# Forty unread matmuls and a new order of the first 337 steps in a linear-attention and ELU kernel

## The chip, the cores and the metric

The kernel runs on one core of one Trainium2 chip. The metric is the time of one execution on the device, in microseconds (us). Engines are named as in the profile: PE is TensorE (its weight loads are PEld), DVE is VectorE, ACT is ScalarE, POOL is GpSimd, SP is SyncE. Each engine works through its own instructions in order; semaphores make one wait for another.

## What is computed

Queries, keys and values have 8 batches, 8 heads, 576 positions and 64 dimensions. Queries and keys go through a feature map of 2 x 128 exponentials, attention is linear in these features, and the result of all heads, one row of 512 per position, goes through two dense layers with an ELU between them.

```python
def phi(x):
    proj = np.einsum('bhsd,df->bhsf', x, w_phi)
    proj = proj - np.max(np.abs(proj), axis=-1, keepdims=True)
    return np.concatenate([np.exp(proj), np.exp(-proj)], axis=-1)
q_p, k_p = (phi(q), phi(k))
kv = np.einsum('bhsf,bhsd->bhfd', k_p, v)
z = np.sum(k_p, axis=2)
out = einsum('bhsf,bhfd->bhsd', q_p, kv) / (einsum('bhsf,bhf->bhs', q_p, z)[..., None] + 1e-06)
...
h = x @ w_in                                  # x: 4608 x 512, w_in: 512 x 2048
g = np.where(h > 0.0, h, np.exp(np.minimum(h, 0.0)) - 1.0)
return g @ w_out                              # w_out: 2048 x 512
```

## The kernel before

The work is cut into 16 groups of four heads of one batch (n = 0 to 15; groups 2b and 2b+1 belong to batch b) for the attention, and 9 chunks of 512 rows for the dense layers, each with 16 slices of the hidden width (jt). All of it runs in one interleaved stream. The string ORDER lists 1,797 steps; each letter calls the next instance of one function, a digit gives the PSUM bank (of 8) that it writes, and a star picks the other engine for a copy. The string fixes each engine's order of instructions; every data and buffer dependence becomes a semaphore wait.

The steps that matter for the first 60 us, with their letter and the line at which the profile shows them:

- a, start: loads w_phi on the queues of SP and ACT, clears mhl[0], mhl[1] and w_pad on DVE, and makes the identity on POOL. b, weights: one cast on DVE (L182), two on ACT (L187). c and d: the selection matrices on DVE (L192, L201).
- e, f, g: loads of k, q and v, issued by POOL (L209); the first batch comes in pieces. h: the two halves of w_in (L218). i: w_out (L221). POOL's loads share one queue and are served in its order; a load also waits for the one eight places before it, whose semaphore it takes over.
- j and l: PE transposes of k and q of the groups 0 to 3 (L233), in a first and a second block of the nine 128-column pieces. k and m: the copies out of PSUM (L240), on DVE, or on ACT with a star.
- A: projection of k (L287), in three thirds per group. B: two exponentials of each third on ACT (L298). C: the maxima on DVE (L305). D: exponentials of the maxima on ACT (L315). E: v times these on POOL (L324), four per group. F: two casts per group on POOL (L333).
- M: projection of q with positions on partitions (L361). N: its maxima on DVE (L388). O: the split of the maxima in two bf16 parts in mhl (L414, L415). P: their transpose (L421). Q: its copy (L426).
- S: projection of q with features on partitions, and the maxima subtracted by matmuls with the selection matrices (L469, L481). T: two exponentials on ACT (L493).
- U: kv of a group in two halves (L509), V: its copy (L519). W: features times kv (L558). X: the division on DVE (L572 to L575). Y and Z: transposes of the result and copies (L623, L633, L640), which make the columns of the dense layers' input xT; Z is on DVE, or on ACT with a star.
- p: the first dense layer for one slice (L665), in 256 columns for chunk 0 and 512 later. q: its exponential on ACT (L676), r: the minimum on POOL (L681), s: the rest of the ELU on DVE (L685). t: the second dense layer, four of its 16 matmuls at a time (L693). u, v: copy and store.

A step is named below by its letter and its instance: S1,0 is the first piece of group 1, U1,1 the second half of kv of group 1, T1,1,0 the first exponential of the second piece of group 1. Copies and divisions read PSUM; a step that writes a bank waits until all who read what was there are done. In the groups 0 and 1 the maxima of the first piece stay in their bank until the split has read them.

Of the kernel before, what the change touches and what calls it, by code (L numbers as in the profile page):

```python
# [15 lines left out]


ORDER = """
eeeacj0j5dkk*bA6CA1A3CBBBBDj0kj5kA6CCBBfl0l2BBmmM1NOgDA4BBfl0l7gmm*P1QS2TCDefA0CTM6NOhhgiEEEFFU4
EEUDM2NV*W6XBBP2Q*S4TTM0NM2NFFEU6EEUOP1Qj0j3S4kkM1NV*W6Xl0S2mTTTTl1mY5Z*Y7j6kZOP0W3XQ*S0TTA5Cp2q  # L20
rp7qM3NrssS0TTBp4qA0p3p2CBqrrsj7kl6mqrssM4Np7p3BBM0Np6A4enfDFqrsqrqBrssCp2qp0Y7p3p1rqrZ*O*qrBW6E
sssDqFrl2m*P4Q*p0p5qrXqrEEssM2Np4qrES6TM0NsS2TTTM0NsY6Zp7qrO*sA0A2BBBU4UVCp7qrsp6qrsP5QBt4S0TCp7
qrsp5p6W2XzTW0XDp7EEFqrqrqttA0nS2TTssrsCBp5qrtu*p7p2p3p4t6qrgDBszsqp5qrqS0rstrTsoFsEqp4Tp7rqzS2s
A0rTtEsCToU4qA2BUrzstV*CBW4up7XW0qBt6rXzDBM4FtNzM0M2sA4NvBp7tNqBzrA0sM2O*BCftBENP7t5uQCEDS2M6TtN
FeTS0M6ETtNTEU2S0A6UTCop4VtqTp3rzBsW0qnp4Xrp2qszW0rqu*O*p3DXvBEp5qsvrp7qrszp6rqsFsA0rqM2np4NBEp5
qCrzP3p2rQ*sqp3srqsDp7rqsfp6sqrBp5rsqEsM0qA2p4NBrt7BrsqFS0CgtTsrTS2EM5TNS0toTsTA5U2CTUBS0VvtBW2z
Tt6XTW4uzA0DXS2BtETzCtFETtzBA2M4BS0t7oTCtDTNFtEBvM0A4EM2NBtzNeBU0fu*UA2Cp6Bp5Cqut4rDBsEp7qM2V*r
p6NqEDnW0wstwrqxgM2trNW0FnetxEp5vusS0qM2Rp7syTNp6TFrqS2Rp4qsrTrsp5qsTp7rqysW0qS2xp6rTzrTp4sEzsq
A0U2qCroUrsBp7RV*syA5BCW2p4zxDqW0Eqxp3Brp2rBsRqA0S5qCnt7rTgRtsvTrstBEvsDS3M5TytNzTt2yu*BW3EzS5x
A0tBFzTRM3CtyTNFtzBEwM5S0vU3NTUToA5Vt7BuA0CtCzDtBEW2BtfxBA4p6BRyp3CqDEW0u*wp2qxrBp7FqFsrS0M4TEt6  # L30
NTtrsqtRrsM0ysM3p5NEzp7qNp2rzqsW0rqp4nxrp5qevstrsqsrS0uU2RTUy*S6TzVp4TsW0vqp3xTrp5qoRrsA0qS6p2CT
rp4TsvqsW6qp3rzBrsp5qexBt2rqRS0DA6srotBsytBsyTA3CtETCzW5Dt7FxFBEtBnRM0yA5M3NBztEutNBzEM0wU2CvfUN
DS4V*Et6uW0TvW2xTtxA4M0BntRBW2Nyzp7ECtqt1xFDrup5FsEA2qM6p4NBrp0ECqU6srBUqM2V*tNrA5sS2Bp7swRp4TRC
yqp0TrztqsBtzrqgy*S2u*W5Torp7xDTp1sqS2qRvW5rsTp4rsTp0zyxqW2Fqp7zrsrsA5qvp1gRBxrp4qsBp3rsqyp2Cqrw
zt7sqrsS0EM5sTtnNTrtEDzsS0M3A5TEtCoTt2NFBEA0U3BCURM5Dty*BEVztBNEW3zu*A0S5xBtTt7CTW3RDtxBEA5wM0B
u*FS3ytNBEtTCp2TFuW0qU3xM5rURM0NV*p7yNp4zqsrS5qA0p3sTroCp2Tqsp7qrW4qrsp6DrsBnp3Rqsp2qrvxBt7rzqs
A0S4srBtsBp6y*TCzp3qRp2qrvwtrsqzsDtrTEsvM0A3M5NBp2ENp1qBru*p0qEsvt7qCFrM5p2rsW3NqtrstFsExA0S5Bty
TCt4TRW2By*txzDA0U5BRS2zUyBtEV*zCtuFDEvW0TS5xt7TEzTtu*ETS0U2TFS4UwTtVW0p6xp3qRTRW0rtqyTp2rxp5qs
p4rqRW0rsqp6sursp3yqsp7qrzxp5rqy*zp4qrssW0rzqt6Rrsp3zxp7qy*W0rsqp2xrp5qstrsqtRrsp4systqzRp7rzst5
qtrvsty*tzt7ztvttt4ttp3p2qp1rqstrqsp3rsp2qt1rqsp0rsp3qtrqsp2rsp0qu*p3rqvstrqsup6rvsp5qp3rqsp2rqs  # L40
p6rqstrqst5rsp3p6qp2rqstrqsp3rsp6qutrqvsp7rsp3qp6rqstrqsup7rvst4qutrvstup7vp6qtrqst5rsp7u*p6qvtr
qstrstt7p6p4qtrqsp3rstqtrsp6t4qutruvstvtt7utvttt6tutvtt7u*tvttuv
"""


# [1 line left out]
def kernel(  # L47
# [10 lines left out]
    nc = tc.nc  # L58
# [36 lines left out]
    psum = ctx.enter_context(  # L95
        tc.tile_pool(name="psum", bufs=1, space=bass.MemoryType.PSUM)
    ).tile([P, 8, 512], FP32, name="banks")
# [18 lines left out]
    mhl = [consts.tile([P, 2, D], BF16, name=f"mhl{j}") for j in range(2)]  # L116
# [24 lines left out]

    FIRST = 2
    PLACE_OF = (
        ((0, 1, 5, 6, 2, 3, 4, 7, 8), (0, 1, 4, 5, 2, 3, 6, 7, 8)),
# [23 lines left out]
    def start():  # L170
        w_f32 = epool.tile([P, CHUNK], FP32, name="e_sb")[:, 0:F]
        for par in range(2):
            queue = (nc.sync, nc.scalar)[par]
            queue.dma_start(out=w_f32[par * D:(par + 1) * D, :], in_=w_phi)
        st["w_f32"] = w_f32
        for j in range(2):
            nc.vector.memset(mhl[j], 0.0)
        nc.vector.memset(w_pad, 0.0)
        make_identity(nc, ident)

    def weights():
        nc.vector.tensor_copy(w_sb, st["w_f32"])  # L182


        for par in range(2):
            rows = slice(par * D, (par + 1) * D)
            nc.scalar.copy(w_pad[rows, par, :], st["w_f32"][rows, :])  # L187
# [148 lines left out]
    def m_mm(n, c, bank=None):  # L336
        if n >= JOINED:
# [16 lines left out]
            return  # L354
        own = min(n // FIRST, 1)
        p0, p1 = PIECES[own][c]
# [13 lines left out]
    def m_max(n, c):  # L370
        if n >= JOINED:
# [7 lines left out]
            return  # L379
        p0, p1 = PIECES[min(n // FIRST, 1)][c]  # L380
        if n < FIRST and c == 0:

# [20 lines left out]
    def m_split(n, part, other=False):  # L403
        if n < FIRST:
            p = ((0, 4), (4, NI))[part]
        else:
            p = (0, NI)
        hi = mhl[n % 2][:, :, p[0]:p[1]]
        if n < FIRST and part == 0:
            mq, eng = st["mq0", n], nc.vector  # L410
        else:
            mq = st["mq", n][:, :, p[0]:p[1]]
            eng = nc.gpsimd if (n < PE_TRANSPOSED) != other else nc.vector
        eng.tensor_copy(hi, mq)  # L414
        eng.tensor_tensor(  # L415
            mhl[n % 2][:, :, NI + p[0]:NI + p[1]], mq, hi, op=ALU.subtract
        )
# [311 lines left out]
    def blocks(name, n):  # L729
        cut = 3 if (name, n) == ("k", 0) else 5  # L730
        return [(name, n, 0, cut), (name, n, cut, NI)]
# [21 lines left out]
        k=(t_copy, [x for n in range(PT) for x in blocks("k", n)]),  # L753
# [9 lines left out]
        O=(m_split, m_parts),  # L763
# [5 lines left out]
        x=(x_join, x_thirds), R=(x_rec, x_thirds), y=(x_scale, x_thirds),  # L769
# [45 lines left out]
```

## Time and profile before

| | us |
|---|---|
| median of five runs | 367.29 |
| lowest and highest of them | 365.46, 368.1 |
| the profiled execution | 365.99 |
| its span, first to last instruction | 364.2 |

Busy time in that span:

| engine | us | share |
|---|---|---|
| PE | 347.2 | 95% |
| PEld | 188.0 | 52% |
| DVE | 268.3 | 74% |
| ACT | 252.4 | 69% |
| POOL | 212.4 | 58% |

The page gives busy shares over the whole span; stretches of it can be asked for by themselves, and so can the order in which one engine's groups of instructions began. A row of that order has the start, the length, the line, the operation, its tiles and shapes and the number of instructions, and in brackets the idle time before it and what ended it. A busy PE in it is not PE at its peak, since the ends of matmuls are modelled. The chain of work is followed back from the last instruction, at each step to what released it; "issue" in it is time in which the engine waited for nothing that the profile shows.

The DMA queues moved 39.70 MB; of it 0.49 MB in 30 packets are instructions on the queue that the page calls q8, and 0.13 MB in 16 packets on q14. Up to about 47 us the queue of POOL's loads is never empty; w_out, issued at 11.92, lands at 42.27.

### The profile page before, as it was taken

To read this page: it belongs to the slowest core of one execution; us is meant where nothing else is said; L and a number is where in the kernel's file an instruction comes from. 1 tells how busy PE (TensorE), PEld (TensorE's weight loads), DVE (VectorE), ACT (ScalarE), POOL (GpSimd) and SP (SyncE) were. 2 spreads that over 40 slices of the span, in tenths; PEclk is the share of its full clock that TensorE was granted. 3 is DMA by queue.
4 is the path that set the end of the run, shared out by engine and by line. 5 is a ranking of instruction groups with operands and counts; after the bars stand their busy time and mean duration, and the time that the engine had idled before them with its cause. 6 is when DMAs were issued, how large, how long until landed. Compare 5 with 4: busy or idle time off the path is not lost.

```text
span 364.2 us, 9813 instructions
## 1 busy us (share of the span) xinstructions
PE 347.2 (95%) x3914; PEld 188.0 (52%) x3914; DVE 268.3 (74%) x474; ACT 252.4 (69%) x481; POOL 212.4 (58%) x323
## 2 busy tenths in 40 slices
PE   4878899999999999999999999999999999999994
PEld 2666676655455454545455445544555444444442
DVE  5888986869867899798978899898858814754300
ACT  4988978877897688868976886788676304564220
POOL 8853857277935978485776596556557404543200
PEclk9999999999999999999999999999999999999999
DMA  7999957597797998946987398053120230214142
GB/s 110 199 212 209 208 94 126 88 188 130 116 142 107 161 198 123 162 69 108 190 148 127 50 181 122 4 110 84 41 48 16 33 75 2 59 29 95 23 101 73
DMA packets 68478, 39.70 MB, mean 109 GB/s; under 512 B 48336, under 2 KB 62800, under 8 KB 68432
## 3 DMA queue, kind: packets, MB, share of 16 engines
q0 software_dynamic: 15856, 18.35, 33.1%
q1 hardware_dynamic: 52416, 20.56, 32.8%
q8 instruction: 30, 0.49, 0.6%
q10 hardware_dynamic: 160, 0.16, 0.1%
q14 instruction: 16, 0.13, 0.1%
HBM read 36.77 MB, written 9.44 MB: 127 GB/s over the span
## 4 chain that ended last, share of the span: by engine, by line
PE 84%; DVE 6%; POOL 3%; DMA 2%; issue 2%; ACT 1%; DVEq 0%; ACTq 0%; POOLq 0%
PE banks L693 34%; PE banks L665 32%; PE banks L509 4%; PE banks L542 3%; PE banks L469 3%; PE banks L287 2%; POOL vs L324 2%; DMA vn<-in_v_dram 2%; PE banks L346 2%; PE banks L558 2%; DVE gT L685 2%; DVE mk L305 1%; DVE mq L388 1%; PE banks L481 1%; PE banks L361 1%
## 5 line engine op out<-in xcount | busy, mean ns | idle before, releaser
L681 POOL TENSOR_SCALAR e_sb<-e_sb 128x512 f32<-128x512 f32 (+1 forms) x160 | 90.7, 572 | 96.7 <-ACT e_sb L676 94.5
L693 PE MATMUL banks<-w_out_sb,gT 128*128 128x512 bf16 x576 | 138.2, 380 | 0.0
L685 DVE SCALAR_TENSOR_TENSOR gT<-e_sb,banks 128x512 bf16<-128x512 f32 (+1 forms) x160 | 96.7, 627 | 44.9 <-POOL e_sb L681 44.4
L676 ACT ACTIVATE e_sb<-banks 128x512 f32<-128x512 f32 (+1 forms) x160 | 87.6, 563 | 60.3 <-PE banks L665 57.0
L665 PE MATMUL banks<-xT,w_in_sb 128*128 128x512 bf16 (+1 forms) x576 | 122.9, 356 | 1.0 <-DVE mq L388 0.9
L665 PEld LDWEIGHTS <-w_in_sb 128*128 128x128 bf16 x640 | 58.9, 98 | 58.6 <-issue 2.7
L298 ACT ACTIVATE EK<-banks 128x768 bf16<-128x768 f32 x96 | 75.3, 814 | 13.0 <-PE banks L287 11.4
L693 PEld LDWEIGHTS <-gT 128*128 128x128 bf16 x576 | 52.5, 98 | 59.8 <-issue 1.9
L324 POOL TENSOR_TENSOR vs<-vn,em 128x576 bf16<-128x576 bf16 x64 | 73.3, 1156 | 15.8 <-ACT em L315 15.7
L493 ACT ACTIVATE Eq<-banks 128x768 bf16<-128x768 f32 (+2 forms) x96 | 73.3, 813 | 9.6 <-PE banks L481 6.1
L305 DVE TENSOR_REDUCE mk<-banks 128x6 f32<-128x768 f32 x48 | 45.3, 952 | 7.4 <-ACT EK L298 4.0
L374 DVE TENSOR_REDUCE mx<-banks 128x6 f32<-128x768 f32 (+1 forms) x30 | 30.7, 1039 | 4.8 <-PE banks L346 3.8
L608 POOL TENSOR_TENSOR xj<-xs,recj 128x448 bf16<-128x448 f32 (+1 forms) x22 | 20.0, 913 | 13.9 <-DVE recj L603 10.6
L703 ACT COPY o_sb<-banks 128x512 f32<-128x512 f32 x23 | 13.4, 591 | 14.6 <-PE banks L693 14.6
L587 DVE TENSOR_TENSOR xs<-banks,e 128x455 f32<-128x455 f32 (+1 forms) x30 | 18.1, 602 | 7.2 <-PE banks L542 5.8
L509 PE MATMUL banks<-vs,EK 64*128 64x65 bf16 x1152 | 22.6, 191 | 0.8 <-POOL vs L324 0.4
L509 PEld LDWEIGHTS <-EK 64*128 64x128 bf16 x1152 | 20.7, 94 | 3.4 <-issue 2.3
L542 PEld LDWEIGHTS <-Eq 128*128 128x128 bf16 x400 | 16.2, 97 | 7.3 <-issue 1.3
L592 DVE TENSOR_TENSOR xs<-banks,xs 128x455 f32<-128x455 f32 (+1 forms) x30 | 18.3, 610 | 1.1
L542 PE MATMUL banks<-kv_sb,Eq 128*128 128x65 bf16 x400 | 17.3, 194 | 0.5 <-DVE kv_sb L519 0.5
L287 PE MATMUL banks<-w_sb,kT 64*128 64x128 bf16 x288 | 17.0, 229 | 0.7 <-ACT kT L240 0.4
L469 PE MATMUL banks<-qT,w_sb 64*128 64x384 bf16 (+2 forms) x102 | 16.3, 324 | 0.9 <-DVE mq L388 0.5
(67 smaller groups left out, 241.8 us busy)
## 6 DMA issues: line engine op xcount, KB each, us to landing
out_dram<-o_sb SPq DMA_DIRECT2D x71, 128.0 KB, 2.4
kn<-in_k_dram POOLq DMA_DIRECT2D x7, 576.0 KB, 8.9
qn<-in_q_dram POOLq DMA_DIRECT2D x7, 576.0 KB, 8.3
vn<-in_v_dram POOLq DMA_DIRECT2D x7, 576.0 KB, 7.8
w_in_sb<-in_moe_w_in_dram POOLq DMA_DIRECT2D x2, 1024.0 KB, 20.0
w_out_sb<-in_moe_w_out_dram POOLq DMA_DIRECT2D x1, 2048.0 KB, 32.2
qn<-in_q_dram POOLq DMA_DIRECT2D x2, 288.0 KB, 7.1
vn<-in_v_dram POOLq DMA_DIRECT2D x2, 288.0 KB, 7.9
```

The source lines that it names most:

```text
L298: nc.scalar.activation(EK[:, sg, 6 * c:6 * c + 6, :].rearrange("p (i r) f -> p r i f", r=2), st["pk", n, c], ACT.Exp, scale=1.0 - 2.0 * sg,)
L305: nc.vector.tensor_reduce(mk[:, 6 * c:6 * c + 6].rearrange("p (i r) -> p r i", r=2), st["pk", n, c], axis=AX.X, op=ALU.max, apply_absolute ...
L324: nc.gpsimd.tensor_tensor(get(("vs", n), new_vs)[:, sg, r, 0:D], st["v", n // 2][:, 2 * (n % 2) + pr], st["em", n][:, sg, r].unsqueeze(2). ...
L374: nc.vector.tensor_reduce(mq.rearrange("p (v r) -> p r v", r=2)[:, :, v0:v1], st["pm", n, c][:, :, 0:v1 - v0, :], axis=AX.X, op=ALU.max, a ...
L493: nc.scalar.activation(Eq[:, sg, :, :, p0 * D:p1 * D].rearrange("p h r x -> p r h x"), st["pq", n, c][:, :, 0:(p1 - p0) * P].rearrange("p ...
L509: nc.tensor.matmul(kv[:, hi, pr, sg, :], EK[rows, sg, pr * NS + s, :], vs[rows, sg, pr * NS + s, :], start=(s == 0), stop=(s == NS - 1),)
L542: nc.tensor.matmul(pn[:, sg, v - v0, :], Eq[:, sg, hi, par, i0 * D:(i0 + 2) * D], kv_sb[:, hi, pr, sg, :], start=True, stop=True,)
L665: nc.tensor.matmul(ph, w_in_sb[:, ct, jt * P:(jt + 1) * P], xT_of(ch)[:, ct, h0:h1], start=(ct == 0), stop=(ct == N_CT - 1),)
L676: nc.scalar.activation(e_sb, st["ph", ch, jt, h0], ACT.Exp)
L681: nc.gpsimd.tensor_scalar(e_sb, e_sb, 1.0, 0.0, op0=ALU.min, op1=ALU.max)
L685: nc.vector.scalar_tensor_tensor(gT[:, jt, h0:h1], st["e", ch, jt, h0], -1.0, st["ph", ch, jt, h0], op0=ALU.add, op1=ALU.max,)
L693: nc.tensor.matmul(po, st["gT", ch][:, jt, tt * P:(tt + 1) * P], w_out_sb[:, jt, :], start=(jt == 0), stop=(jt == N_JT - 1),)
```

## The change

Two things change; no step is added to or taken from ORDER, and from the 338th of its 1,797 steps on it is as it was.

First, start() gets 40 matmuls of a 128 x 16 piece of mhl[0], which was just cleared, with itself. They write 16 x 16 zeros to bank 7, which nothing reads before the next writer. In PE's order they stand ahead of the first transpose.

Second, the first 337 steps are in another order, with other banks. On PE, A0,0 comes ahead of the second block of transposes, S0,0 after U0,0 and U0,1 instead of before them, and U1,0 and U1,1 after S0,1 instead of before P0,1. On POOL, the load of w_out goes from ahead of the first v scaling to behind the last split of group 1, the second v load behind the first four scalings. On DVE the cast of w_sb is first, ahead of c and d. Eleven copies change engines. From DVE to ACT: the copies of k 0,0 (first block), k 1 (both blocks), k 3 (second block) and q 2 (first block), V2 and Q3. From ACT to DVE: k 0 (second block), q 1 (second block), V0 and Z0,0.

```diff
 ORDER = """
-eeeacj0j5dkk*bA6CA1A3CBBBBDj0kj5kA6CCBBfl0l2BBmmM1NOgDA4BBfl0l7gmm*P1QS2TCDefA0CTM6NOhhgiEEEFFU4
-EEUDM2NV*W6XBBP2Q*S4TTM0NM2NFFEU6EEUOP1Qj0j3S4kkM1NV*W6Xl0S2mTTTTl1mY5Z*Y7j6kZOP0W3XQ*S0TTA5Cp2q
...
+eeeabcdj1k*A5j3kA0BBBA2CCj7j4k*k*A4A6BDCDCfl1ml0mM0CNOBBBBBBgfl2l3A0P4mmQDCDgefM6NOBBhhFEEEFEgU4
+UVFFEES2TM6M0NNOP5Q*S4j1kP0QTW6XTTj3kS1TTU4M6EEUV*S2TTM0NNOj7kW4l1m*W2XXP7Q*S0iTTA5BY4Y7ZZl2mM3N
...
@@ -141,6 +141,7 @@
+    UNREAD, UNREAD_COLS, UNREAD_BANK = 40, 16, 7
@@ -177,6 +178,12 @@
             nc.vector.memset(mhl[j], 0.0)
         nc.vector.memset(w_pad, 0.0)
         make_identity(nc, ident)
+        zero = mhl[0].rearrange("p r x -> p (r x)")[:, 0:UNREAD_COLS]
+        for _ in range(UNREAD):
+            nc.tensor.matmul(
+                psum[0:UNREAD_COLS, UNREAD_BANK, 0:UNREAD_COLS], zero, zero,
+                start=True, stop=True,
+            )
```

More of the change, by code (lines that the diff above doesn't have):

```diff
@@ L18 @@
 ORDER = """
-eeeacj0j5dkk*bA6CA1A3CBBBBDj0kj5kA6CCBBfl0l2BBmmM1NOgDA4BBfl0l7gmm*P1QS2TCDefA0CTM6NOhhgiEEEFFU4
-EEUDM2NV*W6XBBP2Q*S4TTM0NM2NFFEU6EEUOP1Qj0j3S4kkM1NV*W6Xl0S2mTTTTl1mY5Z*Y7j6kZOP0W3XQ*S0TTA5Cp2q
-rp7qM3NrssS0TTBp4qA0p3p2CBqrrsj7kl6mqrssM4Np7p3BBM0Np6A4enfDFqrsqrqBrssCp2qp0Y7p3p1rqrZ*O*qrBW6E
-sssDqFrl2m*P4Q*p0p5qrXqrEEssM2Np4qrES6TM0NsS2TTTM0NsY6Zp7qrO*sA0A2BBBU4UVCp7qrsp6qrsP5QBt4S0TCp7
-qrsp5p6W2XzTW0XDp7EEFqrqrqttA0nS2TTssrsCBp5qrtu*p7p2p3p4t6qrgDBszsqp5qrqS0rstrTsoFsEqp4Tp7rqzS2s
@@ L24 @@
[L24 to L41, printed above, removed]
@@ L42 @@
-qstrstt7p6p4qtrqsp3rstqtrsp6t4qutruvstvtt7utvttt6tutvtt7u*tvttuv
+eeeabcdj1k*A5j3kA0BBBA2CCj7j4k*k*A4A6BDCDCfl1ml0mM0CNOBBBBBBgfl2l3A0P4mmQDCDgefM6NOBBhhFEEEFEgU4
+UVFFEES2TM6M0NNOP5Q*S4j1kP0QTW6XTTj3kS1TTU4M6EEUV*S2TTM0NNOj7kW4l1m*W2XXP7Q*S0iTTA5BY4Y7ZZl2mM3N
+S0TTCp7p2qql3mA0CBp4p3p6qqrrsDrrqrBBp7ssessM4Np3j2M0p6NFqrsqk*rqrssA4nBp2qY1Z*p0p3qqW6fCrrsBDp1
+l2O*P4Q*sXqp0qm*Errp5p4S6rsssM2M0NNqqS2TTTTY7Zp6p7qqM2A0BBEFrrEssNU4EUV*rsrsO*CA2p6p7qrsP4p5S0BB
+Q*CqrsTTp6t4W2p7W0XXzqqrsttA0nrDEqrssFS2TTCp6p5p7tqqrsp3p2t6BBrEgDu*zsqp5qrqS0rstrTsoFsEqp4Tp7rq
@@ new lines @@
+zS2sA0rTtEsCToU4qA2BUrzstV*CBW4up7XW0qBt6rXzDBM4FtNzM0M2sA4NvBp7tNqBzrA0sM2O*BCftBENP7t5uQCEDS2
+M6TtNFeTS0M6ETtNTEU2S0A6UTCop4VtqTp3rzBsW0qnp4Xrp2qszW0rqu*O*p3DXvBEp5qsvrp7qrszp6rqsFsA0rqM2np4
+NBEp5qCrzP3p2rQ*sqp3srqsDp7rqsfp6sqrBp5rsqEsM0qA2p4NBrt7BrsqFS0CgtTsrTS2EM5TNS0toTsTA5U2CTUBS0Vv
+tBW2zTt6XTW4uzA0DXS2BtETzCtFETtzBA2M4BS0t7oTCtDTNFtEBvM0A4EM2NBtzNeBU0fu*UA2Cp6Bp5Cqut4rDBsEp7q
+M2V*rp6NqEDnW0wstwrqxgM2trNW0FnetxEp5vusS0qM2Rp7syTNp6TFrqS2Rp4qsrTrsp5qsTp7rqysW0qS2xp6rTzrTp4s
+EzsqA0U2qCroUrsBp7RV*syA5BCW2p4zxDqW0Eqxp3Brp2rBsRqA0S5qCnt7rTgRtsvTrstBEvsDS3M5TytNzTt2yu*BW3Ez
@@ new lines @@
+S5xA0tBFzTRM3CtyTNFtzBEwM5S0vU3NTUToA5Vt7BuA0CtCzDtBEW2BtfxBA4p6BRyp3CqDEW0u*wp2qxrBp7FqFsrS0M4T
+Et6NTtrsqtRrsM0ysM3p5NEzp7qNp2rzqsW0rqp4nxrp5qevstrsqsrS0uU2RTUy*S6TzVp4TsW0vqp3xTrp5qoRrsA0qS6
+p2CTrp4TsvqsW6qp3rzBrsp5qexBt2rqRS0DA6srotBsytBsyTA3CtETCzW5Dt7FxFBEtBnRM0yA5M3NBztEutNBzEM0wU2C
+vfUNDS4V*Et6uW0TvW2xTtxA4M0BntRBW2Nyzp7ECtqt1xFDrup5FsEA2qM6p4NBrp0ECqU6srBUqM2V*tNrA5sS2Bp7swR
+p4TRCyqp0TrztqsBtzrqgy*S2u*W5Torp7xDTp1sqS2qRvW5rsTp4rsTp0zyxqW2Fqp7zrsrsA5qvp1gRBxrp4qsBp3rsqy
+p2Cqrwzt7sqrsS0EM5sTtnNTrtEDzsS0M3A5TEtCoTt2NFBEA0U3BCURM5Dty*BEVztBNEW3zu*A0S5xBtTt7CTW3RDtxBE
@@ new lines @@
+A5wM0Bu*FS3ytNBEtTCp2TFuW0qU3xM5rURM0NV*p7yNp4zqsrS5qA0p3sTroCp2Tqsp7qrW4qrsp6DrsBnp3Rqsp2qrvxB
+t7rzqsA0S4srBtsBp6y*TCzp3qRp2qrvwtrsqzsDtrTEsvM0A3M5NBp2ENp1qBru*p0qEsvt7qCFrM5p2rsW3NqtrstFsEx
+A0S5BtyTCt4TRW2By*txzDA0U5BRS2zUyBtEV*zCtuFDEvW0TS5xt7TEzTtu*ETS0U2TFS4UwTtVW0p6xp3qRTRW0rtqyTp2
+rxp5qsp4rqRW0rsqp6sursp3yqsp7qrzxp5rqy*zp4qrssW0rzqt6Rrsp3zxp7qy*W0rsqp2xrp5qstrsqtRrsp4systqzR
+p7rzst5qtrvsty*tzt7ztvttt4ttp3p2qp1rqstrqsp3rsp2qt1rqsp0rsp3qtrqsp2rsp0qu*p3rqvstrqsup6rvsp5qp3r
+qsp2rqsp6rqstrqst5rsp3p6qp2rqstrqsp3rsp6qutrqvsp7rsp3qp6rqstrqsup7rvst4qutrvstup7vp6qtrqst5rsp7
@@ L43 @@
+u*p6qvtrqstrstt7p6p4qtrqsp3rstqtrsp6t4qutruvstvtt7utvttt6tutvtt7u*tvttuv
 """
```

## The prediction

> **What bounds the kernel now.** First I read the split of the span into stretches, then the order of work on each engine in the first 60 us, then the chain of work there. The columns of the stretches are the length, the busy time and instructions of PE, PEld, DVE, ACT and POOL, the granted clock, the DMA share and GB/s.
>
> ```profile
> 16.60:30.00 13.40, 11.17 (x304) 9.15 (x303) 11.11 (x25) 10.35 (x21) 6.73 (x13) 1.00 1.15 211
> 30.00:46.00 16.00, 13.48 (x180) 9.98 (x179) 15.00 (x32) 15.00 (x37) 11.67 (x23) 1.00 1.23 208
> 46.00:60.00 14.00, 14.00 (x219) 10.07 (x220) 10.92 (x26) 11.16 (x26) 7.32 (x15) 1.00 0.57 100
> 60.00:300.00 240.00, 239.17 (x2843) 125.15 (x2840) 196.23 (x338) 180.14 (x338) 153.08 (x220) 1.00 0.70 109
> ```
>
> From 46 to 300 us PE is busy 253.2 of 254.0 us: it is the bound, and what the change does is worth as much as it moves the moment at which PE fills up. Before 46 us no single engine is full. From 30 to 46 us DVE and ACT are each busy 15.0 of 16.0, so their load is the limit there; from 16.6 to 30 DVE has 2.3 us free, ACT 3.0, PE 2.2. Those gaps come from steps that stand in line in the wrong place, and an order can win them back.
>
> The chain of work shows where (start, length, what):
>
> ```profile
> 4.50 7.13 DMA vn<-in_v_dram
> 11.92 1.15 POOL w_out_sb L221
> 13.09 1.48 POOL vs L324 x2
> ...
> 19.30 3.28 POOL vs L324 x3
> 22.58 0.04 issue
> 22.62 0.47 PE banks L509 x18
> ...
> 26.60 0.64 issue
> 27.23 0.22 PE banks L623
> ```
>
> V lands at 11.64, but POOL issues w_out's load first (1.15 us) and starts scaling v at 13.09; PE's last kv matmuls (L509) wait for POOL until 22.62, and the next projections of q stand behind them in PE's order. Then PE halts for 0.64 us at 26.60 with no wait that the profile shows. ACT pays:
>
> ```profile
> 27.23 0.22 PE L623 MATMUL banks<-ident,xp 128*128 128x128 bf16 x1 [0.64 <-issue]
> 27.88 0.27 ACT L426 COPY mT<-banks 128x128 bf16<-128x128 bf16 x1 [0.64 <-PE banks L421]
> 29.02 1.51 ACT L493 ACTIVATE Eq<-banks 128x768 bf16<-128x768 f32 x2 [0.88 <-PE banks L481]
> q8 instruction: 1, 0.02, 3.0%
> ```
>
> The last line is from the DMA view of 24.5 to 26.5 us: one packet of instructions came in just ahead of the halt. The page counts 30 such packets with 0.49 MB, so 16.4 KB each, against 7,828 PE instructions: about 260 instructions a packet. That this halt is the sequencer at the end of a packet is my reading; the row shows only that the two stand together.
>
> **The unread matmuls.** PE is idle from 0.67 us to 4.53, when k lands. The 40 matmuls need only the memset of mhl[0] (DVE, 0.82 to 1.00). Cheapest row: kv matmuls of 65 columns, 72 in 1.15 us, 16 ns each. Dearest that pipelines: cold transposes of 128 columns, 9 in 1.14 us, 0.107 apart. So they end between 1.6 and 5.3 us: from nothing up to 0.8 us of delay. With 16 columns the first row is the nearer; nothing, covered by the wait for k. Without that cover they'd cost their 0.6 to 4.3 us. Queued behind their wait is only the first transpose, which waits for k anyway.
>
> What they may buy is speed in the first matmuls. These three rows have the same operation and count:
>
> ```profile
> 7.91 1.14 PE L233 MATMUL banks<-ident,kn 128*128 128x128 bf16 x9
> 13.12 1.15 PE L233 MATMUL banks<-ident,qn 128*128 128x128 bf16 x9
> 23.13 0.67 PE L233 MATMUL banks<-ident,kn 128*128 128x128 bf16 x9
> ```
>
> The early ones take 1.7 times as long, although the clock column reads 1.00 throughout. If the fast pace held from 4.53 us, each hop through PE on the early path (transposes of k and q, two or three projections) saves 0.15 to 0.3 us; about 0.4 us reaches ACT and DVE. Bounds: 0 and 0.8. PE was already busy 9.74 of 12.1 us from 4.5 to 16.6 and stayed slow through the 13.12 row, so I take 0 from matmuls this short. [...]
>
> **The new head.** I took every engine's new order of steps and walked it by hand with the rows' spacings: ACT 0.70 per exponential of 768 columns, 0.95 of 1024; DVE 0.87 per maximum of 768, 1.25 of 1024, 0.33 per ELU step; POOL 1.11 per v scaling; PE 0.056 per transpose, 0.27 per projection of k, 0.44 per x matmul group; loads land as now (k 4.49, 5.32 and 7.87, q 10.21, v 11.64, q 13.07, v 14.53, next k 17.35). The stations:
>
> - First exponential (ACT L298): 7.58 now. New order: 3 transposes at 4.53, their copy now first on ACT until 5.5, projection, ready at 6.0. ACT starts 1.6 us earlier; but it takes over two copies of k (1.25), gives up one of q and one of kv (1.2), and waits until 15.95 for the last maximum of group 1.
> - DVE: w_sb's cast fits before the identity is made (3.1 to 3.5), its maxima start at 6.8 against 6.59, run without the k copies between them, and the second split (L414 for group 1) ends at 17.55 against 18.62: 1.1 earlier, though DVE then takes kv_copy(0) (0.65).
> - POOL: v scaling at 11.7 against 13.09. Its eight scalings and four casts (9.4 us) and the two inserted steps (0.75 load issue, 0.5 split) end it at 22.2 against 22.57, but U1,1 (L509) no longer stands before the next q projections.
> - ACT ends the second pair of q exponentials (L493, 128x1024) at 21.5 against 23.00, and starts T1,1,0 at 26.5 against 29.02. Of these 2.5 us about 0.9 is the halt at 26.60, if it goes.
> - DVE ends X0,1 (L575) at 27.2 against 30.08, but has Z0,0 more (0.42): 2.4 earlier.
> - DVE starts N2,1 (L388) at 33.4 against 35.85; from there to 47.4 it is as full as before. ACT, with 1.2 us more copies, ends T2,1,1 at 43.8 against 45.84, and PE enters its full stretch 2.0 to 2.4 us earlier with the same work behind it.
>
> So I take 2.4 with fast early matmuls, 2.0 without.
>
> Moved issues: w_out's load goes from 11.92 to about 23 on POOL. w_in and the next v stand ahead of it in that queue until 29.26 and 32.14, so it still lands near 42.3; first use 48.53 now, some 46.5 then: 4 us of cover, and if a gap opened in the queue its length beyond that would count. The second v load moves from 10.49 to 16.3, also behind w_in. The loads for k and q of batch 2 (34.85, 35.71) stay behind w_out; SP's order doesn't change. The copies that change engines are in the sums above. New waits: S0,0 now stands behind U0,1, which waits for POOL until 16.3; ACT's first q exponential moves from 15.71 to 17.6, and what fills the place on ACT is group 1's last exponentials; 0.85 us of ACT idles before them, already counted.
>
> After a gain, the next late thing is PE itself: 253 us of work that nothing here touches.
>
> **Packets.** The 40 matmuls are 80 PE instructions. The halt stood between the 705th and 706th recorded PE instruction; the packet before it by the same distance near 456. Counted so, the ends fall in S1,0 and S0,2 of the new order. [...] From packet to restart took 27.23 - 24.94 = 2.3 us (the packet's start in the trace). Cost here: between 0, when the waits cover both, and 2 x 2.3 = 4.6 when neither is covered and ACT waits for all of it. The observed halt let through 0.64, near the cover end; I take 0 in the forecast since the waits at U0,1 and U1,1 are longer than those before 26.60. [...]
>
> **Sum.** Profiled execution: 365.99 us with a span of 364.2, so 1.8 lies around it. It is 1.3 below the median 367.29, and five runs spread over 365.46 to 368.1. 365.99 - 2.0 = 364.0 in its own terms; against the median 367.29 - 2.0 = 365.3. A measurement here tells 0.5% (1.84 us) from no change, so the forecast is barely a gain.
>
> **Rivals.**
> - *Forecast*, 2.0 to 2.4 us gained, 365.0 to 365.3: chance 0.40.
> - *The early clock opens and all hops gain*: the 0.8 bound and a POOL order with no idle; 3.3 gained, 364.0. For it: nine transposes lose 0.47 us cold. Against: three groups of nine within 9 us didn't speed up. 0.08.
> - *Packet ends bite in part*: at S1,0 and S0,2 ACT waits 0.5 to 1.0 at each, 0.3 to 1.2 us remain, 366.1 to 367.0; no measurable change. For it: the sequencer's lead over PE is small where kv matmuls run 16 ns apart. Against: the waits for POOL. 0.30.
> - *Packet ends uncovered* (slower): same place, both halts in full, 4.6 - 2.0 = 2.6 lost, 369.9; with one later halt uncovered as well 372. It turns into a loss once the two let through over 1.0 us each, into a measurable one from 1.9 each. For it: at 26.60 the sequencer reached the end when only 39 instructions were left to run. 0.20.
> - *Unread matmuls don't pipeline*: 40 x 0.289 (one isolated transpose) = 11.6, ending 8 us after k lands; 373. Decides from 88 ns each (3.53 / 40). Against: w_in matmuls into one bank run 0.11 apart, not 0.27. 0.02.
>
> Chances: faster by over 0.5% 0.40 + 0.08 = 0.48; within 0.30; slower 0.20 + 0.02 = 0.22. The range takes in the first three and the slower case up to 1.7 us beyond the median: 363.3 to 369.0; what is left is about 0.14 above and 0.04 below. The forecast's own range is 364.3 to 366.3.
>
> **What would show it.** Right: first L298 near 6.0, v scaling near 11.7, no issue idle on PE near S1,0 and S0,2, the 9-transposes rows at 1.14 until about 13 us, X0,1 done near 27, the 48.53 L693 row near 46.3. Wrong: ACT waiting for L481 behind an issue idle on PE; w_out landing after 46; full PE only from 46 us on; or a stretch after 60 us that is no longer full, which nothing in this sum allows.

## The result and the profile after

The changed kernel takes 370.14 us (median of 28 runs, 366.42 to 375.41), the kernel before on the same chips 366.51 (47 runs, 365.46 to 371.08). The ratio is 1.0068, with an interval of 1.0047 to 1.0088: slower by about 2.5 us. Executions over 1.5% above the fastest of their kernel are left out of the ratio, which makes it smaller than that of the medians, and the profiled execution of after, 373.68 us with a span of 371.9, is one of them, so that its readings are held below against other kernels' profiles. The loss isn't in every execution: of the 28 runs 15 lie above 369.5 and 6 below 367, of the 47 of the kernel before 4 lie above 369.5. The forecast was 365.3.

The same four stretches of the span, with the columns as before:

```profile
16.60:30.00 13.40, 12.52 (x315) 10.26 (x311) 11.47 (x26) 11.37 (x19) 7.55 (x13) 1.00 1.15 211
30.00:46.00 16.00, 13.75 (x175) 10.54 (x172) 15.25 (x32) 14.67 (x36) 11.57 (x23) 1.00 1.23 208
46.00:60.00 14.00, 13.94 (x221) 9.87 (x218) 10.42 (x24) 11.49 (x29) 6.87 (x14) 1.00 0.54 92
60.00:300.00 240.00, 234.13 (x2810) 123.01 (x2808) 195.43 (x337) 180.60 (x340) 154.17 (x221) 0.99 0.70 107
```

Up to 30 us PE gets more done (315 matmuls against 304), but from 30 to 46 no more than before (175 against 180). The loss is in the last row: from 60 to 300 us, where the order is unchanged, PE is busy 5.0 us less (234.13 against 239.17). Cut finer, first the kernel before, then the kernel after:

```profile
130.00:140.00 10.00, 9.96 (x163) 5.67 (x161) 9.60 (x19) 8.98 (x18) 7.70 (x12) 1.00 1.18 170
140.00:150.00 10.00, 9.77 (x124) 5.02 (x123) 8.84 (x15) 8.45 (x16) 8.21 (x11) 1.00 1.03 158
```

```profile
130.00:140.00 10.00, 5.24 (x77) 3.13 (x76) 4.53 (x9) 4.48 (x8) 4.95 (x7) 0.83 1.28 140
140.00:150.00 10.00, 10.00 (x108) 4.98 (x102) 8.01 (x18) 7.78 (x15) 5.52 (x8) 0.83 0.48 88
```

Nearly all of it (4.7 us) lies between 130 and 140 us. The granted clock is 0.83 in both stretches: after the idle time PE runs at a lower clock, and from 140 to 150 it is busy throughout for 108 matmuls where it did 124. The DMA engines are busier (1.28 against 1.18) and move less (140 GB/s against 170). What PE waits for is in the chain of work of after:

```profile
114.67 8.53 DMA kn<-in_k_dram
123.22 15.29 DMA kT<-kn
138.51 0.05 issue
138.56 0.50 PE banks L294 x6
```

K of batch 4 takes 8.53 us to load; then the DMA transposes of group 8's k (ORDER's letter n, issued by SP) take 15.29 us, and PE stands until 138.56. In the kernel before the same two took 7.35 and 9.4 us and PE didn't wait: the first transpose, of group 8, landed at 130.62, 2.3 us ahead of the projection that needs it. From its DMA view (KB, us to landing) and PE's order of work:

```profile
kn<-in_k_dram POOLq DMA_DIRECT2D x1, 576.0 KB, 7.3
...
kT<-kn SPq DMA_TRANSPOSE x1, 9.4
```

```profile
132.89 0.34 PE L287 MATMUL banks<-w_sb,kT 64*128 64x128 bf16 x6
```

"Transposes" below means this first one.

The order of work on PE in the head (lines in after stand 7 further down than in before):

```profile
0.99 1.16 PE L183 MATMUL banks<-mhl 128*16 128x16 bf16 x40 [0.99 <-DVE mhl L178]
...
8.42 1.14 PE L240 MATMUL banks<-ident,kn 128*128 128x128 bf16 x9
...
26.25 0.44 PE L240 MATMUL banks<-ident,qn 128*128 128x128 bf16 x5
26.56 0.92 PE L565 MATMUL banks<-kv_sb,Eq 128*128 128x65 bf16 x24
27.31 0.22 PE L428 MATMUL banks<-ident,mhl 128*128 128x128 bf16 x1
```

The unread matmuls end at 2.15 us, 27 ns apart, and delay nothing. Nine transposes at 8.42 still take 1.14. The halt that stood at 26.60 is gone.

### The profile page after: what moved, and what is told of

Its sections match the earlier page's. It is cut to its first block, busy times and chain, and to the rows that moved or that the text cites. A ratio compares the mean times of both kernels' runs of the same rounds, so it can differ in the third digit from the quotient of the medians.

```text
span 371.9 us, 9890 instructions
## 1 busy us (share of the span) xinstructions
PE 351.4 (94%) x3954; PEld 191.5 (51%) x3954; DVE 268.2 (72%) x471; ACT 253.8 (68%) x484; POOL 213.2 (57%) x323
## 4 chain that ended last, share of the span: by engine, by line
PE 78%; DMA 8%; DVE 7%; ACT 3%; issue 2%; SPq 1%; POOL 0%; DVEq 0%; ACTq 0%; POOLq 0%
PE banks L700 30%; PE banks L672 29%; PE banks L516 5%; DMA kT<-kn 4%; DMA kn<-in_k_dram 3%; PE banks L549 3%; PE banks L294 3%; PE banks L476 3%; PE banks L565 2%; ACT Eq L500 2%; DVE gT L692 2%; PE banks L353 1%; DVE mk L312 1%; DMA qT<-qn 1%; PE banks L368 1%
## 5 line engine op out<-in xcount | busy, mean ns | idle before, releaser
L516 PE MATMUL banks<-vs,EK 64*128 64x65 bf16 x1152 | 23.9, 197 | 0.1
L516 PEld LDWEIGHTS <-EK 64*128 64x128 bf16 x1152 | 22.3, 99 | 2.3 <-issue 1.5
L294 PEld LDWEIGHTS <-kT 64*128 64x128 bf16 x288 | 9.9, 99 | 18.4 <-issue 10.4
```

The costliest lines, as they stand in the source:

```text
L294: nc.tensor.matmul(pj[:, par, i3, :], st["kT", n][rows, 3 * c + i3, :], w_sb[rows, :], start=True, stop=True,)
L516: nc.tensor.matmul(kv[:, hi, pr, sg, :], EK[rows, sg, pr * NS + s, :], vs[rows, sg, pr * NS + s, :], start=(s == 0), stop=(s == NS - 1),)
```

## The experiments

A run's time is a median; beside it stands that of the kernel before on the same chip.

| run | us | before | ratio, interval |
|---|---|---|---|
| new order, 40 unread (the change) | 370.14 | 366.51 | 1.0068, 1.0047 to 1.0088 |
| e3_no_unread: new order, none | 367.86 | 366.49 | 1.0046, 1.0014 to 1.0079 |
| e4_unread_only: old order, 40 | 371.43 | 366.49 | 1.0113, 1.0063 to 1.0162 |
| e1_later: the change, two loads moved | 367.54 | 366.49 | 1.0018, 0.9993 to 1.0043 |
| e5_unread_later: old order, 40, loads moved | 366.55 | 366.65 | 0.9981, 0.9950 to 1.0012 |
| e6_before_later: old order, none, loads moved | 366.77 | 366.65 | 1.0005, 0.9976 to 1.0034 |
| e8_port: e1 and one v scaling moved | 366.35 | 366.65 | 1.0005, 0.9970 to 1.0040 |
| e12_order_clean: e8 without unread | 367.61 | 366.37 | 1.0035, 1.0016 to 1.0055 |
| e7_unread_128: old order, 128 | 367.66 | 366.65 | 0.9999, 0.9971 to 1.0027 |
| e11_after_128: new order, 128 | 367.97 | 366.37 | 1.0039, 1.0006 to 1.0072 |
| e9_unread_40_88: old order, 40 and 88 later | 368.60 | 366.37 | 1.0065, 1.0043 to 1.0087 |
| e10_unread_mid: old order, 40 at 96 us | 372.71 | 366.37 | 1.0163, 1.0113 to 1.0213 |

### Which part loses, and are the loads the place?

Two runs take the change apart. `UNREAD = 0` in the kernel after (e3), and start()'s added lines alone in the kernel before (e4).

> The changed kernel without the 40 unread matmuls; the new order stays. If the unread matmuls do harm (theory B1): 366 to 367. If they do nothing (theory A, and my forecast of 0 for them): as the changed kernel, 368 to 371, with the wait near 130 us still there in most executions; the ends of the instruction packets fall 80 PE instructions later in the order, which may add up to 2.3 us in the head.

> The kernel before with the 40 unread matmuls alone. Theory A: within 0.3% of before, 365.5 to 367.5, less up to 0.7 if the halt near 26.6 us goes with the shifted packets. Theory B1 (the unread matmuls do harm, by the clock or by the packets): 368 to 371.

The unread matmuls alone lose more than the whole change (371.43), the new order alone some 1.4 us (367.86). In e4 the head is 0.71 us earlier than before at 56 us (four matmuls of the second dense layer that start at 55.80 in the kernel before start at 55.09); what is lost comes later. The waits of e4 from 128 to 142 us (total, times, longest):

```profile
PE banks L294 <- DMA kT<-kn: 4.5, 1, 4.5
```

That is the stall of after, with the old order, in an execution of 371.19 us. The transposes took 16.1 us here, and 4.9 in e3, where PE doesn't wait for them. Beside them in the DMA engines run loads that POOL issues. Two of those were moved, v of batch 4 (letter g) and k of batch 5 (letter e):

```diff
-...nW0wstwrqxgM2trNW0FnetxEp5vusS0qM2Rp7syTNp6TFrqS2Rp4qsrTrsp5q...
+...nW0wstwrqxM2trNW0FntxEp5vusS0qM2Rp7syTgNp6TFrqS2Rp4qsrTresp5q...
```

> The changed kernel, with two POOL loads of the unchanged part of the order issued later: v of batch 4 (122.40 us in the profile after) behind 6,0's scaling step, some 4 us later, and k of batch 5 (123.97) some 6 us later. Theory A (the transposes of k for group 8, issued at 123.22, land 15.3 us later since the two loads stand beside them in the DMA engines; PE then waits 4.8 us): the transposes land in 4 to 6 us, no wait of PE there, the time falls to 366 to 367.5 and its spread to some 1.5 us. Theory B (the loss is made in the first 60 us or by the unread matmuls): the time stays near 370 with the same spread.

> The kernel before plus the 40 unread matmuls, with the load of v of batch 4 moved behind the sixth group's first x scaling and the load of k of batch 5 behind the next minimum but one (some 4 to 6 us later on POOL's queue). Theory (the loss of the unread matmuls is the transposes of group 8's k colliding with these two loads): the transposes land in 3 to 5 us, PE doesn't wait at 132 to 137 us, and the 0.7 us won in the head stays: 365.8 us, 0.7 under the kernel before. Rival (the unread matmuls cost by themselves, for example by where the instruction packets of PE fall, and the transposes are late for the same reason): the stall moves or stays and the time is 369 to 371, as with the unread matmuls alone.

> The kernel before with only the two loads moved. Theory (in the kernel before the collision just fits into the slack of the transposes): no change of the median, 366.0 to 366.8, transposes of group 8's k landing in 3 to 5 us instead of 9.4. Rival (the later loads make v or k of the next batches late, which would be the reason why the new order with the same move stayed at 367.5): 367.5 or more, with a stall of PE at 150 to 200 us.

In all three the transposes land within 3.8 to 4.5 us and PE doesn't wait for k at 133. With the loads moved the 40 matmuls cost nothing in the old order (366.55; without them 366.77), but of the 0.7 us that they had won in the head in e4 only 0.2 shows, which the intervals don't tell from nothing. The change itself comes back to 367.54; the profiled execution of e1 (372.04 us; nine of its 12 runs lie below 368.3) has another wait for a DMA, for the transposes of xj, in its waits from 190 to 200 us (f1 below has it with 1.8 us, f4 with 3.1, so there is a second such place):

```profile
PE banks L672 <- DMA xT<-xj: 3.0, 1, 3.0
```

Moving v's load the other way, 1.2 us earlier in the kernel before (`...qM2V*rp6N...` to `...qM2V*rgp6N...`), was to provoke the stall:

> The kernel before, with one load moved: v of batch 4 issued some 1.7 us earlier (119.8 instead of 121.55), so that it stands ahead of the transposes of k for group 8 (121.18). Theory A: the transposes land 13 to 16 us after their issue instead of 9.4, PE waits some 3 to 6 us, the time rises to 369 to 373. Theory B: no change, 366 to 367.

It did not: 367.41, ratio 1.0008 (0.9984 to 1.0033; two of the 12 runs lie above 371), transposes 8.3 us with v's load issued 1.25 us ahead of them. "V's load ahead of the transposes" is too simple a theory.

### Why do 40 matmuls at 1 us delay a DMA at 120?

Behind the head two things differ in e4: all work is some 0.7 us earlier, and 80 more PE instructions stand ahead of everything else. With about 260 of them to an instruction packet (the prediction's estimate; the kernel after has 7,908 and 31 packets, so about 255), 80 more should move the end of every later packet. In the profile of before packets came between 110.5 and 110.6 us and between 122.5 and 122.6, on both sides of the flight of k's load (113.82 to 121.18); in that of after between 108.8 and 108.9 and between 120.5 and 120.6, the second in the flight (114.67 to 123.20). 128 unread matmuls are 256 instructions, by that estimate nearly one packet, and should move the ends back; and the 40 can be put where the head is over:

```diff
     def h_mm(ch, jt, h0, h1, bank=None):
+        if (ch, jt) == (1, 14):
+            piece = ident[:, 0:16]
+            for _ in range(40):      # 88 in e9_unread_40_88
+                nc.tensor.matmul(
+                    psum[0:16, bank, 0:16], piece, piece, start=True, stop=True,
+                )
```

> The kernel before with 128 unread matmuls: 256 PE instructions, about one instruction packet, so that the ends of the later packets fall nearly where they fell without any; at 27 ns each they end near 4.5 us, when k lands. Theory A (what the 40 did was to shift the ends of the packets): the halt at 26.60 us is back, the transposes of group 8's k land in about 9 us, and the time is 366.5 to 367. Theory B (any unread matmuls in front do it, or the moment alone): stall of 4 to 5 us again, 370 to 371.5. Beside it, the clock: if 3.5 us of such matmuls open the early clock, the first groups of nine transposes take 0.67 us instead of 1.14 and the head is 0.4 us or more earlier at 26 us; if not, 1.14.

> The kernel before with 40 unread matmuls only ahead of the dense layer's slice at about 96 us: the head is that of the kernel before to the instruction, only the packet ends after 96 us are shifted by 80 instructions. They cost 40 x 27 ns = 1.1 us. Theory A (packet ends): transposes of group 8's k late, stall of 4 to 5 us, 371 to 373. Theory B (the head): no stall, 366.65 + 1.1 = 367.5 to 368.0.

> The kernel before with 40 unread matmuls at the start and 88 more ahead of one slice of the dense layer at about 96 us, 256 PE instructions in all, so that the ends of the instruction packets fall after 100 us where they fall in the kernel before. PE is full there, so the 88 cost 88 x 27 ns = 2.4 us, and everything later, the loads too, moves by the same. Theory A (from the 40 matmuls it is the shifted packet ends that bring the late transposes): no stall of 3 us or more at 130 to 140 us; 366.65 + 2.4 less what the head wins (0 to 0.7) = 368.3 to 369.1. Theory B (it is the head that runs 0.7 us earlier or otherwise, and the DMAs meet differently because of it): the stall of 4 to 5 us stays, 372 to 374.

> The kernel after with 128 unread matmuls instead of 40. Theory A (packet ends): it behaves like the new order without unread matmuls (367.86), no stall at 133, 367.5 to 368.2. Theory B (the unread matmuls as such, or the moment of the loads in the new order): stall as in the kernel after, 369.5 to 371.

In the time all four go to the side of the packet ends, though not in every detail. e10 has the head of the kernel before, instruction for instruction, and 40 matmuls at 96 us that should cost 1.1; it loses 6.3, and PE waits 5.8 for kT. e7 loses nothing that the ratio can tell, but its median is above the 366.5 to 367 expected (its runs lie in two heaps, 365.8 to 366.5 and 367.6 to 368.6, and one at 372.75; the profile is of the lower heap, and what makes the upper one isn't known). The head has its halt where it had been:

```profile
0.99 3.36 PE L183 MATMUL banks<-mhl 128*16 128x16 bf16 x128 [0.99 <-DVE mhl L178]
...
8.61 1.14 PE L240 MATMUL banks<-ident,kn 128*128 128x128 bf16 x9 [0.55 <-DMA kn<-in_k_dram]
...
27.73 0.22 PE L630 MATMUL banks<-ident,xp 128*128 128x128 bf16 x1 [0.93 <-issue]
```

The same transpose of xp as in the kernel before waits for nothing that the profile shows, now 0.93 us. And 3.36 us of unread matmuls leave the next nine transposes at 1.14: matmuls this short didn't raise the early pace, 40 or 128. e11 behaves like the new order without unread matmuls (367.97 against 367.86), not like the change. e9 meets the number (368.6), though its profiled execution (369.83) has transposes of 13.1 us and a wait of 1.6 us on PE: the packet ends are no switch, but a matter of likelihood.

How the packet gets at the transposes, the DMA views show while k's load is under way (queue lines: packets, MB, share; issues: KB, median us to landing). First e10, then e7:

```profile
q8 instruction: 1, 0.02, 0.7%
...
kn<-in_k_dram POOLq DMA_DIRECT2D x1, 576.0 KB, 8.0
...
kT<-kn SPq DMA_TRANSPOSE x1, 16.9
```

```profile
kn<-in_k_dram POOLq DMA_DIRECT2D x1, 576.0 KB, 7.1
...
kT<-kn SPq DMA_TRANSPOSE x1, 6.2
```

With the shifted ends a packet of instructions is moved during k's load; without, none is. And e5, with the packet there and the two loads out of the way:

```profile
q8 instruction: 1, 0.02, 0.7%
...
kn<-in_k_dram POOLq DMA_DIRECT2D x1, 576.0 KB, 8.4
...
kT<-kn SPq DMA_TRANSPOSE x1, 3.9
```

The load is late there as well, but nothing follows from it. In the ten profiles with a packet in that flight the load took 7.4 to 8.6 us (mean 8.0), in the ten without 6.1 to 8.0 (7.1). The two ranges overlap, and in e4 the load took 7.50, only 0.15 longer than in the kernel before; that the packet is the reason is likely, not shown. In the kernel after the 16th of the load's 16 parts came at 8.53, the 15th at 7.44; in six of the ten with a packet the last part is 0.47 to 1.29 behind the 15th, in none of the ten without more than 0.42. SP issues the transposes when k has landed, POOL issues v's load 7.73 us after k's in every profile that left these loads where they were. So the length of k's load decides which comes first, with a packet in its flight or, as in e9 (7.57 us), without.

| execution | v's load after the transposes' issue, us | next k's load | transposes took |
|---|---|---|---|
| e2 | -1.25 | +2.00 | 8.3 |
| after | -0.82 | +0.75 | 15.3 |
| e10 | -0.25 | +1.31 | 16.9 |
| e9 | +0.15 | +1.71 | 13.1 |
| e4 | +0.21 | +1.78 | 16.1 |
| before | +0.37 | +1.93 | 9.4 |
| e11 | +0.43 | +1.99 | 7.5 |
| e7 | +0.61 | +2.17 | 6.2 |
| e3 | +1.30 | +2.9 | 4.9 |
| e1, e5, e6, e8, e12 | +4.5 to +5.8 | over 7 | 3.8 to 4.8 |

With one profile of each, the kernel before (+0.37) stands 0.2 us from e4 (+0.21), which stalled. e2 doesn't fit the order of the rows. Five runs test this race.

> The kernel after with only the load of k of batch 4 moved, two v scalings ahead on POOL (2.2 us earlier). The instruction packet still falls in its flight or just behind it. Theory (the race): k lands 1.0 to 1.5 us ahead of v's load, the transposes take 5 to 8 us, no stall at 133, 367.0 to 367.8 as without the unread matmuls. Rival (the moved loads helped for another reason than their place against the transposes): stall of 4 to 5 us as in the kernel after, 369.5 to 371.

> The kernel after with only the load of k of batch 5 moved behind (5 us later); v's load stays 0.8 us ahead of the transposes. Theory V (v's load starves the transposes): they still take 12 us or more, stall of 2 to 5 us, 369 to 371. Theory K (it is the second load, which follows v's without a pause, that keeps them from catching up; when v's load was put 1.25 us ahead with the second load 2.0 us behind they took only 8.3 us): transposes 8 to 9 us, no stall, 367.2 to 367.9.

> The kernel after with only the load of v of batch 4 moved behind (4 us later); the load of k of batch 5 stays 0.75 us behind the transposes. Theory V: without v's load in front the transposes start at once, 5 to 8 us, no stall, 367.2 to 367.9. Theory K: the second load, now the first to meet them, starves them as well: 12 us or more, stall of 2 to 5 us, 369 to 371.

> The kernel before, with no unread matmul and the old order, plus two fillings of an unused 128x512 tile on POOL ahead of the load of k of batch 4 (0.6 us each by the row of the minimum of the same width), in a stretch in which POOL is idle for 2 us; so that load is issued some 1.2 us later and the load of v stays where it is. Theory (the race: k's load must land, and its transposes be issued, some 0.3 us ahead of v's load; an instruction packet in its flight makes it land 1 us later): this does without a packet what the packet does; v's load comes 0.8 us ahead of the transposes, they take 15 us, PE stalls 4 to 5 us, 370 to 372. Rival (the packet ends cost in another way and the late landing is a bystander): 366.3 to 367, no stall.

> The kernel before, no unread matmuls, old order, with the load of v of batch 4 1.2 us and the load of k of batch 5 some 1.5 us earlier on POOL: against the transposes of group 8's k they then stand at -1.2 and about +0.4 us (-0.8 and +0.75 in the kernel after, +0.4 and +1.9 in the kernel before; the run with v alone 1.25 us ahead had +2.0 for k and lost nothing). Theory (the loads' moments against the transposes are all that counts; the instruction packets only move them): no pause in the loads' queue, transposes 12 us or more, stall of 3 to 5 us, 369 to 371. Rival (packet ends are needed for the loss): 366 to 367, transposes 8 to 10 us.

Edits of ORDER, each by its letter:

```diff
 f1_k_early (after): k of batch 4 two scalings earlier
-...oTCtDTNFtEBvM0A4EM2NBtzNeBU0fu*...
+...oTCtDTNFetEBvM0A4EM2NBtzNBU0fu*...
 g1_both_early (before): v of batch 4 and k of batch 5 earlier
-...qM2V*rp6NqEDnW0wstwrqxgM2trNW0Fnetx...
+...qM2V*rgp6NqEDnW0wstwreqxM2trNW0Fntx...
 f2_k_late (before), in load(); idle is a new 128x512 tile
+        if (name, b) == ("k", 4):
+            for _ in range(2):
+                nc.gpsimd.memset(idle, 0.0)
```

- f1: 367.07 (before 366.40; ratio 0.9996, 0.9958 to 1.0033). The packet is still there and the load takes 8.2 us, but k lands 1.5 us ahead of v's issue; transposes 5.8 us, no wait at 133. It keeps the packet and the long load and changes only which comes first: the race, not the packet as such.
- f3 (only k of batch 5 moved): 367.57, ratio 1.0024 (0.9994 to 1.0055), with four of the 12 runs above 371. f4 (only v moved): 373.57; five of its six runs lie above 373, too few are left for a ratio. In f3's profile the transposes take 11.5 us beside v's load (+0.06), in f4's 12.1 beside the next k's (-0.18, v at +4.28). Either load alone makes the transposes slow; neither theory V nor theory K holds by itself. What the slow transposes cost is another matter: in f3's profile (366.6) PE starts on kT at 133.46, just when it has landed (133.42), and in f4's (378.9) it waits only 1.2 us for it, with other waits behind it (2.5 us for DVE at 147.7, 3.1 us for xT near 200).
- f2: 366.30, ratio 1.0003 (0.9968 to 1.0038). A failed imitation: issued 0.9 us later the load flew only 6.1 us and the order stayed (+0.47; transposes 6.3).
- g1: 367.23 (before 366.48), ratio 1.0028 (0.9994 to 1.0063). Its DMA view while k's load was under way:

```profile
kn<-in_k_dram POOLq DMA_DIRECT2D x1, 576.0 KB, 6.3
...
vn<-in_v_dram POOLq DMA_DIRECT2D x1, 576.0 KB, 7.4
...
kT<-kn SPq DMA_TRANSPOSE x1, 12.3
```

  No packet in the flight, v at -0.30, and the transposes took 12.3 us, as the theory has it. But they were issued early, at 120.69, landed at 132.99, and PE didn't wait: the expected 369 to 371 was missed in the median; three of the 12 runs lie above 370. The next k's load came at +2.25, not at the +0.4 planned. So the loads' moments alone make the transposes slow; that they alone make the whole stall isn't shown.

### What the new order itself is worth

In the kernel after one step of DVE's split of group 2 took 1.08 us (0.18 in the kernel before), beside a v scaling on POOL. The order of work of all engines in after, then DVE's in e8, where that scaling (E) stands behind the next minimum (r): `...qm*Errp5...` to `...qm*rErp5...`.

```profile
39.33 1.15 POOL L331 TENSOR_TENSOR vs<-vn,em 128x576 bf16<-128x576 bf16 x1
39.43 1.08 DVE L422 TENSOR_TENSOR mhl<-mq,mhl 128x18 bf16<-128x18 f32 x1
```

```profile
39.19 0.33 DVE L422 TENSOR_TENSOR mhl<-mq,mhl 128x18 bf16<-128x18 f32 x1
```

> The kernel after with the two loads moved as in the first such run (367.5 us) and one v scaling of group 2 on POOL one minimum later, so that it no longer runs beside DVE's subtraction in the split of group 2 (1.08 us at 39.43, 0.18 to 0.23 elsewhere). Theory (a port that DVE and POOL share): the subtraction takes 0.2 us, the transpose of the split and all behind it come 0.8 us earlier, and the time falls by 0.5 to 0.9, to 366.6 to 367.0. Rival (DVE or ACT is late there anyway): the subtraction is fast but what follows is not earlier, 367.3 to 367.8.

> The new order without unread matmuls, with the two loads moved and the v scaling one minimum later (the run with 40 unread matmuls took 366.35). Theory (with the collision gone the unread matmuls do little, 0.2 as between the two runs of the old order): 366.3 to 366.7. Rival (the unread matmuls keep a halt at a packet end off the path and are worth the 0.6 to 0.7 of the halt): 366.9 to 367.2.

e8 took 366.35, 1.2 less than e1 (their ratios' intervals overlap), and PE's eight matmuls of the first dense layer near 61 us start at 60.47, 0.8 us earlier than in the kernel before (61.29), where after's start 0.2 later (61.46). In the rows of after DVE's step, begun 0.10 us behind POOL's, ends within 0.03 us of it (40.51 and 40.48); with the scaling moved it takes 0.33. The scaling takes its usual 1.15; so DVE's step is the one held up, by what isn't shown, nor that it is a port, as the theory has it.

e12 went to the rival, and beyond it: 367.61. Without unread matmuls PE halts in the new order too (also in e3, and 0.85 us in e11):

```profile
28.00 0.73 PE L565 MATMUL banks<-kv_sb,Eq 128*128 128x65 bf16 x18 [0.94 <-issue]
```

With the 40 matmuls this halt isn't there (in e8 the 24 matmuls of L565 run through from 26.33 us), and they are worth 367.61 - 366.35 = 1.26 us in the new order: nine of e8's 12 runs lie below 366.7, none of e12's below 367.1, and the matmuls that start at 60.47 in e8's profile start at 61.95 in e12's. They pay in the head and are charged at 133.

### A version with the cause taken away

> The version that the runs point to: the kernel after with 40 unread matmuls, the v scaling one minimum later, and the two loads moved to where POOL has idle time (v behind the fourth minimum of chunk 2, k of batch 5 behind the eleventh), so that they don't delay the minima as in the run of 366.35, whose PE waited 0.74 us at 127.9. Theory: that wait goes, 365.6 to 366.1. Rival (v's load now lands too late for the scalings at 137, or the later k load meets the transposes of the next group): 366.5 or more, with a wait of POOL for v at 137 or of PE behind 150.

g2 put the two loads into POOL's idle time (g behind the fourth minimum of chunk 2, e behind the eleventh) and took 369.97 (before 366.48; ratio 1.0085, 1.0054 to 1.0117): the rival. SP's queue and then PE:

```profile
136.25 1.66 SPq L656 DMA_TRANSPOSE xT<-xj  x1
144.38 1.30 SPq L266 DMA_TRANSPOSE kT<-kn  x1
...
148.64 1.23 SPq L663 DMA_TRANSPOSE xT_last<-xj  x1
149.97 2.24 SPq L656 DMA_TRANSPOSE xT<-xj  x1
```

```profile
158.01 1.24 PE L672 MATMUL banks<-xT,w_in_sb 128*128 128x512 bf16 x5 [2.18 <-DMA xT<-xj]
```

K of batch 5 now lands at 144.33. SP stands in order on its transposes from 137.9 on, the transposes of xj are queued behind them, and PE waits 2.18 us for xT at 158. No version beat the kernel before by what can be measured: the best medians are 366.30 (f2) and 366.35 (e8).

## Why the prediction was wrong, step by step

- **The step that failed** is "After a gain, the next late thing is PE itself: 253 us of work that nothing here touches". The change touches it: with 80 more PE instructions ahead, a packet came at 120.5 us, in the flight of k's load, where in the kernel before the next came at 122.5, behind it. The packets were counted only up to 30 us, as halts of PE, and the later ones, 28 of 30 in the profile of before, were taken to be harmless. What the runs showed in its place: a loss near 133 us in which PE waits for a DMA. With a packet in its flight k's load of batch 4 takes 8.0 us instead of 7.1 on average, v's load then comes ahead of the transposes or 0.2 us behind them, they take 15 to 17 us instead of 9.4, and PE waits 4.5 to 5.8 us for them (after, e4, e10). That it is the shifted ends that bring the stall rests on e10, which has a packet in that flight with the old head and stalls, and on e7 and e11, which have 128 unread matmuls, their order's halt in the head (0.93 and 0.85 us), no packet in that flight and no stall; the link from the packet to the longer load is argued from the means. None of the rivals had this; the one on the slower side named packet ends, but as halts of PE at S1,0 and S0,2, and came nearer in time (369.9) by luck.
- What would refute it was named, "a stretch after 60 us that is no longer full, which nothing in this sum allows", and it came.
- **Unread matmuls**: 0 in the head, ends in the bounds, right (2.15 us). The early pace: 0 from matmuls this short, right for 40 and for 128 (nine transposes at 1.14 us behind either). What sets that pace no run shows; in the kernel after the granted clock reads 1.00 from 0 to 15 us.
- **Packets in the head**: no halt near S1,0 and S0,2 and the one at 26.60 gone, right. That the 40 matmuls are what removes it, and not the order, the prediction didn't separate; e4 (old order with them, no halt) and e12 (new order without, 0.94 us) show it. For the packets the sum takes 0 since PE's waits at U0,1 and U1,1 cover their ends; no run shows such a cover, only that no halt came there.
- **The new head, -2.0**: mis-sized. The first stations were near: first exponential 6.30 (walk 6.0), first v scaling 11.99 (11.7). Then the walk ran away: DVE's first maximum 7.85 (6.8; the copy of k ahead of it waited for PE's second block of transposes until 7.05, and then 0.24 us went by on ACT, which reads the same bank), second split ended at 18.66 (17.55), POOL's eighth scaling at 24.06 (22.2; before 22.57; it waited 1.39 us for DVE), T1,1,0 28.32 (26.5; before 29.02), N2,1 35.05 (33.4; before 35.85). At 39.43 the collision of DVE and POOL took 0.9 more. Measured: +0.2 us at 61 us in the kernel after, -0.8 with the collision taken away (e8). The walk had every engine's spacing, but left out waits between the engines and between readers of one bank, and the collision of DVE and POOL. DVE's first maximum in after:

```profile
7.05 0.56 DVE L247 COPY kT<-banks 128x768 bf16<-128x768 bf16 x1 [1.57 <-PE banks L240]
7.85 0.96 DVE L312 TENSOR_REDUCE mk<-banks 128x6 f32<-128x768 f32 x1 [0.24 <-ACT EK L305]
```

- **w_out**: issued at 26.70 (23 in the walk), landed at 44.03, first used at 50.7 without a wait, right. The 42.27 given for its landing in the kernel before is the eighth of its 16 parts; the last came at 44.14 (in the same way w_in's came at 31.14 and v's at 33.98).

What stays open: why a transpose that meets a load slows so far (3.8 to 16.9 us for the same data) and why it didn't in e2, and whether the packet lengthens the load by sitting in one DMA engine; the late 16th part fits, but f2, meant to imitate the late landing without a packet, failed.

## What to carry to other kernels

Here 40 more matmuls at 1 us came with an instruction packet in the flight of a load at 115 to 123 us, where the kernel before had none; so compare the landing times of loads over the whole span, not only the place that was edited. Before trusting a full engine, look for transfers with little to spare: here 0.2 us in the order of two issues, and 2.3 us between the landing of k's transposes and their use, stood between no wait and one of 4.5 us. A load moved away from one collision is to be followed to the next: who waits for it in order, and who is queued behind that.

## What the runs showed of the hardware

- Two losses came with instruction packets (16.4 KB each, 30 in the profile of before). PE halted 0.59 to 1.21 us with no wait that the profile shows in the ten profiles that have the head's halt (in the kernel before at 26.60, behind a packet that came at 24.94; that this is a packet's end is a reading). And k's load of batch 4 took about 1 us more on average with a packet in its flight (8.0 against 7.1 us, means of ten profiles each; that the packet is the reason isn't shown).
- The first DMA transpose of k took 3.8 to 4.8 us with no load issued within 4 us behind it and 11.5 to 16.9 with one issued within 0.3 us of it or ahead of it, except once, in e2 (8.3 us); while they meet, the DMA engines are busy and move less (105 to 125 GB/s at a busy share of 0.97 to 1.46 from 124 to 133 us in the kernel after, 196 to 197 at 1.18 to 1.25 from 118 to 124).
- 2.8 us into PE's idle time in the kernel after the granted clock went to half and stayed there from 136.6 to 143.4 us; 72 kv matmuls took 1.98 us there and 1.15 at 157.08, so this stall cost more than its length. In e4 it went to half 4.2 us into the idle time, for 3.4 us (mean of the execution 0.994); in e9 a wait of 1.6 us left it at 1.00.
